# First loads, weight preparation and tail of an FFT-mix and top-1 MoE kernel: one constant moved to another queue, a software-pipelined Gram product, and the undecided tokens' list read in two blocks

## The chip, the cores and the metric

The kernel runs on one core of a Trainium2 chip. The metric is the device time of one execution in microseconds; three executions of the kernel before are given, and one of them was profiled. A smaller number is better.

## The reference

```python
X = np.fft.rfft(x, axis=1)                       # x: 8 x 3072 x 256
Yr, Yi = Xr @ w_r - Xi @ w_i + b_r, Xr @ w_i + Xi @ w_r + b_i
Yr, Yi = soft_threshold(Yr, 0.01), soft_threshold(Yi, 0.01)
t = np.fft.irfft(Yr + 1j * Yi, n=3072, axis=1)   # 24576 tokens of 256
r = np.maximum(t @ w_in, 0.0)                    # 256 x 2048
u = (s * (r * r) + b) @ w_out                    # 2048 x 256
e = argmax(u @ w_gate, axis=1)                   # 8 experts, softmax weight g
# each expert takes its first 768 tokens, in order; the others give 0
out[i] = g[i] * (np.maximum(u[i] @ w1[e], 0.0) @ w2[e])
```

The biases b_r and b_i are 64 times their usual size, so nearly all tokens choose the same expert. It is full after the first few hundred tokens, and most of the output is zero.

## The kernel before

**The body.** A batch of 3072 tokens is transformed as 32 x 96: `f1_items` multiplies 16 tiles of x by the matrix `f` (`pz`), writes the result `z` to the DRAM tensor `zd`, and `group_items` reads it back as `zp`, does the second half of the transform, the mix by `w_r` and `w_i` (`wm`) and the threshold. `i2_items` is the inverse transform (`pi`). Each token's row then goes to DRAM (`ad`) and through a first FFN in low precision (`ph`, `r`, `qb`, `lg`).

Which expert a token takes is computed exactly for the first 1024 tokens only. For all others `lg_set`, `lg_out` and `lg_fin` form bounds of the logits, and `decide_items(b)` finds the tokens of batch b whose bounds do not settle whether they go to the full expert. `to_list` writes their numbers to a DRAM list with eight indirect DMAs on POOL, appended to those of earlier batches (`base` is the count). `ovf` says that a batch had more of them in one row than the eight columns hold; in that case `whole_list` builds the whole list again, with 256 indirect DMAs (32 `to_list` steps for each batch).

**Weight preparation, before and in batch 0.** `conv_items(seq, ahead)` prepares the first FFN's weights in pieces: a load of `cr`, `conv_low` on ACT, `conv_use`/`conv_word` on DVE and POOL (`cf`), `conv_tr` (transposes `pwt`), `conv_gate` (`pg`). Pieces 0 to 7 (CONV_B) run among the first steps of batch 0. `gram_items` forms w_in times its transpose from the prepared weights, in 16 tiles: `turn(k, f)` transposes four 128x128 pieces (`pwg`) and ACT copies them to `wgt`; `add(k, f)` does four matmuls from `wgt` (`gram`). The items are put in slots of batch 0, at even distances up to GRAM_TO, in the order of this list:

```python
for k in range(2):
    for f in range(0, NF, 2):
        it += [lambda k=k, f=f: turn(k, f), lambda k=k, f=f: add(k, f)]
```

**First loads.** `run` issues the 16 loads of x for batch 0 on SP (`f1_load`, L214), then `load_consts` the constants, `f` first (L165), also on SP.

**The slots of a batch.** A batch's main loop has steps k; `slot` is a table from step number to work that is put in there. In the last batch it holds, from S_FROM = 27 to S_TO = 62, the sorting of the first 1024 tokens for the full expert, and at 62 `full_rows(j)`, the gathers of that expert's six blocks of 128 rows (`yf`).

**The tail.** Everything after the last batch stands in `tail`. `block(j)` is the full expert's block j: transposes `pt` (L1413), an ACT copy `yT`, 32 matmuls `ph` (L1423), 16 matmuls `po` (L1433), scatter `out` (L1438); its ten steps are [a, b x4, c x4, d]. `among(main, side)` spreads the steps of `side` among those of `main`. The order is: blocks 0 and 1 with `decide_items` of the last batch among them; `whole_list` (a branch on `ovf`, L884 and L888); `ids()`, which loads the list (`ci`) and makes row numbers of 512 entries on DVE (L1523 to L1532); four gathers `ga` of 128 rows (`x_load`); block 2; two parts (`e2_steps`) that recompute 256 listed tokens each exactly; block 3 with `xroute_items`, which counts them in; `e2_more`, which loads the list's count into a register and branches over a loop for lists of more than 512; blocks 4 and 5 with the tables of the other experts' tokens (`final_tables`, last `pit` and the cast `eo` on DVE, L1316). The loads of five experts' weights (`w`, `wb`, two `wq`, `wa`) and the gathers of their rows are issued from these. `regs()` then loads the two counts, and two nested chains of branches follow:

```python
with self.tc.If(self.nblk > n):    # item(n): block of 128 tokens of one expert
    ...
    if n + 1 < NI:
        self.item(n + 1)
with self.tc.If(self.nsml > NQ * g):  # small(g): three experts of up to 32
```

With these inputs items 0 and 1 and the group small(0) run. Matmuls on fp32 operands are used there. DRAIN instructions of every engine end the program (L1875).

## Time and profile before

| | |
|---|---|
| median of three executions | 1651.17 us (1646.57 to 1651.53) |
| profiled execution, its own time | 1647.89 us |
| its span | 1646.1 us |
| mean granted TensorE clock | 0.966 |
| TensorE busy (share of the span) | 89% |
| VectorE, ScalarE, GpSimd busy | 58%, 49%, 16% |

The span is the time from the first to the last instruction of the profiled execution. The shares are averages over stages that have different limits; so what a stage costs is read from its own waits and windows. A wait names the engine and line that stood still and what came last to release it. PEclk is the granted clock, 1.00 being 2.4 GHz and 0.50 1.2 GHz. "q" behind an engine's name is its sequencer, which runs branches, register loads and semaphores.

### The profile page before, as it was taken

To read this page: it belongs to the slowest core of one execution; us is meant where nothing else is said; L and a number is where in the kernel's file an instruction comes from. 1 tells how busy PE (TensorE), PEld (TensorE's weight loads), DVE (VectorE), ACT (ScalarE), POOL (GpSimd) and SP (SyncE) were. 2 spreads that over 40 slices of the span, in tenths; PEclk is the share of its full clock that TensorE was granted. 3 is DMA by queue.
4 is the path that set the end of the run, shared out by engine and by line. 5 is a ranking of instruction groups with operands and counts; after the bars stand their busy time and mean duration, and the time that the engine had idled before them with its cause. 6 is when DMAs were issued, how large, how long until landed. Compare 5 with 4: busy or idle time off the path is not lost. (4 is left out here: it accounts for less than half of the span.)

```text
span 1646.1 us, 26007 instructions
## 1 busy us (share of the span) xinstructions
PE 1471.8 (89%) x9469; PEld 1217.3 (74%) x9469; DVE 953.6 (58%) x2057; ACT 814.1 (49%) x1252; POOL 268.1 (16%) x235
## 2 busy tenths in 40 slices
PE   6986789999998799999999999999999988988865
PEld 3875568777877568867876887788688768977753
DVE  1856357645555767755765676577557686633510
ACT  1425544563334564476457446744764575632311
POOL 0534100110000040021012001300220161231020
PEclk9997999999999899999999999999999999999978
DMA  7635454562443365465446435644655347610035
GB/s 208 236 107 169 131 153 153 158 185 100 148 135 123 87 152 152 122 171 150 147 135 166 143 122 159 175 128 131 166 146 153 91 110 229 183 50 17 14 105 180
DMA packets 273572, 230.03 MB, mean 140 GB/s; under 512 B 120045, under 2 KB 228335, under 8 KB 273424
## 3 DMA queue, kind: packets, MB, share of 16 engines
q1 hardware_dynamic: 255776, 200.17, 42.5%
q10 hardware_dynamic: 13824, 25.17, 4.1%
q0 software_dynamic: 3824, 2.82, 0.7%
q8 instruction: 80, 1.31, 0.4%
q14 instruction: 68, 0.56, 0.1%
HBM read 114.18 MB, written 114.09 MB: 139 GB/s over the span
## 5 line engine op out<-in xcount | busy, mean ns | idle before, releaser
L723 PE MATMUL ph<-ah,win 128*128 128x384 f32 (+1 forms) x2048 | 489.5, 367 | 8.4 <-ACT r L728 7.8
L728 ACT ACTIVATE r<-ph 128x768 bf16<-128x768 f32 (+1 forms) x512 | 395.6, 784 | 165.9 <-PE ph L723 123.2
L729 DVE TENSOR_TENSOR qb<-r 128x768 bf16<-128x768 bf16 (+1 forms) x512 | 298.9, 585 | 298.2 <-ACT r L728 270.5
L723 PEld LDWEIGHTS ph<-ah,win 128*128 128x128 f32 x2048 | 344.9, 192 | 79.9 <-issue 41.6
L335 PE MATMUL pmx<-wm,l 128*128 128x256 f32 x1196 | 296.5, 386 | 17.1 <-DVE kb L345 9.6
L398 POOL TENSOR_TENSOR asq<-ah 128x768 bf16<-128x768 f32 x64 | 95.9, 1498 | 1045.7 <-ACT ah L394 967.5
L335 PEld LDWEIGHTS pmx<-wm,l 128*128 128x128 f32 x1196 | 220.9, 191 | 54.1 <-DVE kb L345 16.0
L392 PEld LDWEIGHTS pi<-f1t,u 96*128 96x128 f32 x1024 | 129.6, 196 | 17.8 <-issue 8.9
L392 PE MATMUL pi<-f1t,u 96*128 96x96 f32 x1024 | 134.1, 281 | 6.7 <-DVE l L262 4.3
L226 PE MATMUL pz<-x,f 96*96 96x512 f32 x240 | 126.6, 612 | 14.6 <-DMA f<-c_f 14.6
L261 ACT COPY l<-pf 128x512 f32<-128x512 f32 x84 | 49.2, 586 | 142.7 <-PE pf L253 142.3
L373 ACT COPY v<-pi 128x512 f32<-128x512 f32 x96 | 56.3, 587 | 125.5 <-PE pi L371 125.5
L371 PE MATMUL pi<-t,e 128*128 128x256 f32 x384 | 99.7, 383 | 5.2 <-DVE t L330 5.2
L253 PEld LDWEIGHTS pf<-d,zp 128*128 128x128 f32 x672 | 88.9, 193 | 11.6 <-issue 3.8
L253 PE MATMUL pf<-d,zp 128*128 128x128 f32 x672 | 90.0, 277 | 6.9 <-DMA zp<-zd 6.9
L408 DVE STREAM_TRANSPOSE at<-pi 128x384 f32<-128x384 f32 x128 | 74.1, 579 | 34.6 <-ACT ah L394 24.8
L394 ACT CAST ah<-pi 128x384 fp32r<-128x384 f32 x128 | 61.1, 479 | 57.3 <-PE pi L392 57.3
L234 ACT COPY z<-pz 96x512 f32<-96x512 f32 x120 | 69.8, 581 | 37.7 <-PE pz L226 29.8
L371 PEld LDWEIGHTS pi<-t,e 128*128 128x128 f32 x384 | 72.7, 191 | 17.6 <-DVE t L330 7.0
L330 DVE TENSOR_TENSOR t<-t,cl 128x512 f32<-128x512 f32 x96 | 72.1, 752 | 3.3
L877 POOL DMA_INDIRECT list<-c,x x64 | 65.9, 1029 | 45.1 <-DVE c L873 29.0
L759 ACT COPY ls<-lg 128x384 f32<-128x384 f32 (+1 forms) x64 | 52.8, 825 | 25.7 <-PE lg L746 15.5
(395 smaller groups left out, 1814.5 us busy)
## 6 DMA issues: line engine op xcount, KB each, us to landing
zd<-z SPq DMA_DIRECT2D x128, 192.0 KB
zp<-zd SPq DMA_DIRECT2D x96, 256.0 KB
vd<-v ACTq DMA_DIRECT2D x96, 256.0 KB
u<-vd SPq DMA_DIRECT2D x64, 384.0 KB
ad<-at SPq DMA_DIRECT2D x256, 96.0 KB
out<-zero SPq DMA_DIRECT2D x96, 256.0 KB
x<-x SPq DMA_DIRECT2D x120, 192.0 KB
sd<-stage SPq DMA_DIRECT2D x32, 256.0 KB
```

The costliest lines, as they stand in the source:

```text
L226: nc.tensor.matmul(o, self.f1, xs.rearrange("p a c -> p (a c)"), start=True, stop=True)
L234: nc.scalar.copy(out=z.rearrange("p a c -> p (a c)"), in_=o)
L253: nc.tensor.matmul(pv[:, h, :, gi * 64:gi * 64 + 64], zp[:, gi, h * 128:(h + 1) * 128], self.d[:, 2 * p + gi, :].rearrange("p (t m) -> p t ...
L330: nc.vector.tensor_tensor(out=t, in0=t, in1=cl, op=ALU.subtract)
L335: self.nc.tensor.matmul(o, part(h), w[:, h], start=start and h == 0, stop=stop and h == 1, skip_group_check=True)
L371: nc.tensor.matmul(ps[:, gi * C:(gi + 1) * C], self.e[:, 2 * p + gi], t[:, gi * C:(gi + 1) * C], start=True, stop=True)
L392: nc.tensor.matmul(ps[:, :TC].rearrange("p (a n) -> p a n", n=4)[:, :, n], u[:, n, h::2], self.f1t, start=True, stop=True)
L398: nc.gpsimd.tensor_tensor(out=self.asq[b, i], in0=af, in1=af, op=ALU.mult)
L408: nc.vector.transpose(out=self.ar[:, :, :, h], in_=self.at.pop((b, i, h))[:, :TC].rearrange("p (g c) -> p g c", c=32))
L723: nc.tensor.matmul(ps[:, j, :n], self.win[:, k, f], ah[:, k, t0:], start=(k == 0), stop=(k == 1))
L728: nc.scalar.activation(out=r, in_=ps[:, :, :n], func=AF.Relu)
L729: nc.vector.tensor_tensor(out=q, in0=r, in1=r, op=ALU.mult)
```

## The change

- `f` is loaded on ACT's queue, ahead of everything else, instead of on SP's behind x.
- `conv_items` gets a parameter `early`: for CONV_B the loads stand three steps ahead instead of two, and `conv_low` and `conv_word` two ahead instead of one. For this the buffer of `f` there takes turns with that of `t`.
- `gram_items`: `turn` of the next tile stands ahead of `add` of the one before; `wgt` has two buffers that take turns, and `gsq` another one.
- `first_block`, in slot 60 of the last batch, loads the first 256 entries of the list as they then are and gathers their rows (two `ga`). The tail begins with the recomputation of these (`part(0)`), with `decide_items` of the last batch among its steps. `whole_list` also rebuilds the list when fewer than 256 entries were there (`early`), and then does part 0 again (`redo`). The second 256 entries are gathered after it; block 0 and `part(1)` follow. The register load of `e2_more` goes ahead of block 0 (`e2_count`); its branch stays where `xroute_items` end.
- Blocks 1 and 2, and 3 to 5, are interleaved by `line`: the next block's first step goes ahead of this one's `po`.
- Items 0 and 1 (interleaved in the same way) and the first small group run without a branch; `regs()` and the chains of branches, from item 2 and from small group 1 on, come behind them.

The diff; in `small` the body is moved to `small_do` with the same lines, which are left out:

```diff
@@ -123,6 +123,7 @@
 S_FROM = 27
+LIST_AT = 60
 S_TO = 62
@@ -161,8 +162,6 @@
     def load_consts(self, cp):
         nc, I = self.nc, self.I
-        self.f1 = cp.tile([N1, 96], F32, tag="f1", name="f1")
-        nc.sync.dma_start(out=self.f1, in_=I["c_f1"])
         self.f1t = self.mo.tile([96, N1], F32, tag="f1t", name="f1t")
@@ -496,7 +495,7 @@
             pool = self.wk
-            tag, n = dict(t=("z", 4), p=("sl", 2), m=("v", 3), f=("zp", 3))[what]
+            tag, n = dict(t=("z", 4), p=("sl", 2), m=("v", 3), f=(("zp", "t")[k % 2], 3))[what]
         return pool.tile([128, 512], dt, tag=tag, name="c" + what, bufs=n)
     def conv_load(self, k):
@@ -583,18 +582,18 @@
-    def conv_items(self, seq, ahead):
+    def conv_items(self, seq, ahead, early=1):
         def at(f, n):
...
             at(self.conv_load, n + ahead)
-            at(self.conv_low, n + 1)
+            at(self.conv_low, n + early)
             for f, lag in ((self.conv_use, 0), (self.conv_tr, 1), (self.conv_gate, 2)):
...
                     f(seq[n - lag])
-            at(self.conv_word, n + 1)
+            at(self.conv_word, n + early)
         return [lambda n=n: step(n) for n in range(-ahead, len(seq) + (2 if seq[-1] < 8 else 0))]
     def load_bias(self, pp):
@@ -627,25 +626,27 @@
                                     (self.win, self.wl)[k].bitcast(F32)[:, c, (f + ff) * 128:(f + ff + 1) * 128], self.ident)
-            t = self.wk.tile([128, 2, 2 * 128], F32R, tag="kw", name="wgt", bufs=1)
+            t = self.wk.tile([128, 2, 2 * 128], F32R, tag=("kw", "kw2")[f // 2 % 2], name="wgt", bufs=1)
             nc.scalar.copy(out=t.rearrange("p a c -> p (a c)"), in_=ps)
-            self.wgt = t
+            self.wgt[k, f] = t
...
                 self.gram = self.lp.tile([128, 512], F32, tag="lg", name="gram")
+            t = self.wgt.pop((k, f))
             for ff in range(2):
                 for c in range(2):
-                    nc.tensor.matmul(self.gram[:, c * 256:(c + 1) * 256], self.wgt[:, ff, c * 128:(c + 1) * 128], self.wgt[:, ff],
+                    nc.tensor.matmul(self.gram[:, c * 256:(c + 1) * 256], t[:, ff, c * 128:(c + 1) * 128], t[:, ff],
                                      start=(f + ff == 0 and c == 0), stop=(f + ff == NF - 1), skip_group_check=True)
             if f == NF - 2:
-                sq = self.wk.tile([128, 512], F32, tag="kw2", name="gsq", bufs=1)
+                sq = self.wk.tile([128, 512], F32, tag="lh", name="gsq", bufs=2)
                 nc.scalar.activation(out=sq, in_=self.gram, func=AF.Square)
                 nc.vector.tensor_reduce(out=self.nrm[:, k:k + 1], in_=sq, axis=AX.X, op=ALU.add)
-        it = []
-        for k in range(2):
-            for f in range(0, NF, 2):
-                it += [lambda k=k, f=f: turn(k, f), lambda k=k, f=f: add(k, f)]
+        self.wgt = {}
+        tiles = [(k, f) for k in range(2) for f in range(0, NF, 2)]
+        it = [lambda: turn(*tiles[0])]
+        for n, t in enumerate(tiles):
+            it += [lambda u=u: turn(*u) for u in tiles[n + 1:n + 2]] + [lambda t=t: add(*t)]
         return it
     def bound_items(self, pp, diff=False):
@@ -802,7 +803,7 @@
         self.cnt, self.base = zero("cnt", [E]), zero("base", [1])
-        self.cmax = zero("cmax", [1])
+        self.cmax, self.early = zero("cmax", [1]), zero("early", [1])
         self.T = zero("T", [5, 48])
@@ -878,10 +879,13 @@
-    def whole_list(self):
+    def whole_list(self, redo):
         nc, V = self.nc, self.nc.vector
-        ovf = nc.values_load(self.ovf[0:1, 0:1], min_val=0, max_val=128)
+        V.tensor_scalar(out=self.early, in0=self.early, scalar1=float(TD), scalar2=None, op0=ALU.is_lt)
+        V.tensor_tensor(out=self.ovf, in0=self.ovf, in1=self.early, op=ALU.add)
+        ovf = nc.values_load(self.ovf[0:1, 0:1], min_val=0, max_val=129)
@@ -908,6 +912,7 @@
                     self.to_list(n, x, c)
+            redo()
     def x_load(self, ga, ids):
@@ -1443,76 +1448,81 @@
     def item(self, n):
         with self.tc.If(self.nblk > n):
-            if n > 1:
-                self.load_item(n)
-                self.rows(self.yr[n % 2], self.idy[:, n:n + 1])
-                self.gate(n)
-            for f in self.block_steps(self.wx[n % 2], self.yr[n % 2], self.gg[n % 2], self.ids[:, n:n + 1], "o2"):
+            self.load_item(n)
+            self.rows(self.yr[n % 2], self.idy[:, n:n + 1])
+            self.gate(n)
+            for f in self.item_steps(n):
                 f()
...
+    def item_steps(self, n):
+        return self.block_steps(self.wx[n % 2], self.yr[n % 2], self.gg[n % 2], self.ids[:, n:n + 1], "o2")
     def small_load(self, g, *qs):
...
     def small(self, g):
+        P = 32 * NQ
+        with self.tc.If(self.nsml > NQ * g):
+            self.small_load(g, *range(NQ))
+            self.rows(self.nr[:P], self.nids[:, 2, g:g + 1])
+            self.gather(self.ng[:P], self.gd, self.nids[:, 0, g:g + 1])
+            self.small_do(g)
+            if g + 1 < NS:
+                self.small(g + 1)
+    def small_do(self, g):
         nc, pq = self.nc, self.pq
...
@@ -1543,15 +1553,26 @@
-    def e2_more(self, p2, again):
-        nc, tc, V = self.nc, self.tc, self.nc.vector
-        bi, rem, blk = self.rt("e2i", [1], I32), self.rt("e2r", [1]), self.rt("e2b", [2])
+    def e2_count(self):
+        nc, V = self.nc, self.nc.vector
+        bi, rem = self.rt("e2i", [1], I32), self.rt("e2r", [1])
         V.tensor_scalar(out=rem, in0=self.base, scalar1=float(TD - 1), scalar2=None, op0=ALU.add)
...
         V.tensor_scalar(out=bi, in0=bi, scalar1=8, scalar2=None, op0=ALU.arith_shift_right)
-        n = nc.values_load(bi[0:1, 0:1], min_val=0, max_val=(self.B * S - XT) // TD)
+        self.nlist = nc.values_load(bi[0:1, 0:1], min_val=0, max_val=(self.B * S - XT) // TD)
+    def first_block(self):
+        c = self.e2_ids(2, self.list[0:TD], None, self.base)
+        self.nc.vector.tensor_copy(out=self.early, in_=self.base)
+        self.first_rows = self.x_load(self.gbuf[0], c[3])
+    def e2_more(self, p2, again):
+        nc, tc, V = self.nc, self.tc, self.nc.vector
+        rem, blk = self.rt("e2r", [1]), self.rt("e2b", [2])
+        n = self.nlist
         with tc.If(n > SB):
@@ -1610,33 +1631,40 @@
-        def load(k):
-            x[k] = self.x_load(self.gbuf[k % 2], x["c"][3][:, 2 * k:2 * k + 2])
         def among(main, side):
...
         self.lg_fin(B - 1, 7)
+        lg = self.rt("e2g", [2 * SB, E])
+        def part(k, rows):
+            return self.e2_steps(lambda: rows, lg, 2 * k, self.yx[XT + TD * k:XT + TD * (k + 1)])
+        def redo():
+            c = self.e2_ids(2, self.list[0:TD], None, self.base)
+            for f in part(0, self.x_load(self.gbuf[0], c[3])):
+                f()
+        def line(blocks):
+            it = [f for f in blocks[0][:5]]
+            for n, b in enumerate(blocks):
+                nx = blocks[n + 1] if n + 1 < len(blocks) else []
+                it += nx[:1] + b[5:] + nx[1:5]
+            return it
         blocks = [block(j) for j in range(NJ)]
-        among(blocks[0] + blocks[1], self.decide_items(B - 1))
-        self.whole_list()
+        among(part(0, self.first_rows), self.decide_items(B - 1))
+        self.whole_list(redo)
         ids()
-        for k in range(min(SB, 2)):
-            load(k)
-        lg = self.rt("e2g", [2 * SB, E])
-        for f in blocks[2]:
+        rows = self.x_load(self.gbuf[1], x["c"][3][:, 2:4])
+        self.e2_count()
+        for f in blocks[0] + part(1, rows):
             f()
-        for k in range(SB):
-            st = self.e2_steps(lambda k=k: x[k], lg, 2 * k, self.yx[XT + TD * k:XT + TD * (k + 1)])
-            st.pop(0)()
-            if k + 2 < SB:
-                load(k + 2)
-            for f in st:
-                f()
         hf, lf, val, row = x["c"]
         side = self.xroute_items(2 * SB, lg, lambda: hf, lambda: lf, lambda: x["b"], self.gdv[:, XB:XB + 2 * SB], val)
-        among(blocks[3], side)
+        among(line(blocks[1:3]), side)
@@ -1646,10 +1674,13 @@
         self.wx = [self.wx[1], cut(wb)]
-        among(blocks[4] + blocks[5], tables)
+        among(line(blocks[3:]), tables)
+        for f in line([self.item_steps(n) for n in range(2)]):
+            f()
+        self.small_do(0)
         regs()
-        self.item(0)
-        self.small(0)
+        self.item(2)
+        self.small(1)
     def run(self):
@@ -1687,6 +1718,8 @@
             nc.vector.memset(zero, 0.0)
+            self.f1 = cp.tile([N1, 96], F32, tag="f1", name="f1")
+            nc.scalar.dma_start(out=self.f1, in_=self.I["c_f1"])
             for t in range(16):
@@ -1714,7 +1747,7 @@
                 if not conv:
-                    conv = self.conv_items(CONV_B, 2)
+                    conv = self.conv_items(CONV_B, 3, 2)
             self.warm(WARM_GROUPS)
@@ -1779,6 +1812,7 @@
                     slot.setdefault(S_TO, []).extend(lambda j=j: self.full_rows(j) for j in range(NJ))
+                    slot.setdefault(LIST_AT, []).append(self.first_block)
                     self.yf = [p2.tile([128, C], F32, tag=f"yf{j}", name=f"yf{j}") for j in range(NJ)]
...
```

TensorE where the Gram product begins in batch 0 (`ph` is the first FFN, `pwt` a transposition of `conv_tr`), before:

```order
L723 MATMUL ph<-ah,win 128x256 x4
L569 MATMUL pwt<-ident,cf 128x128 x4
L628 MATMUL pwg<-ident,win 128x128 x4
L639 MATMUL gram<-wgt 128x256 x4
L628 MATMUL pwg<-ident,win 128x128 x4
L639 MATMUL gram<-wgt 128x256 x4
L723 MATMUL ph<-ah,win 128x256 x4
```

and with the change:

```order
L724 MATMUL ph<-ah,win 128x256 x4
L627 MATMUL pwg<-ident,win 128x128 x8
L639 MATMUL gram<-wgt 128x256 x4
L627 MATMUL pwg<-ident,win 128x128 x4
L724 MATMUL ph<-ah,win 128x256 x4
L568 MATMUL pwt<-ident,cf 128x128 x4
L639 MATMUL gram<-wgt 128x256 x4
L627 MATMUL pwg<-ident,win 128x128 x4
```

The eight transposes at the start are those of two tiles. From there on each group of four Gram matmuls has the transposes of the next tile ahead of it, where before its own stood directly ahead.

VectorE at the register load of the list's count, before (`T` is the last step of `xroute_items`, L1120):

```order
L1120 TENSOR_TENSOR T<-ptb,T 128x240
L1551 TENSOR_SCALAR e2r<-base 128x1
L1552 CAST e2i<-e2r 128x1
L1553 TENSOR_SCALAR e2i<-e2i 128x1
L1554 TENSOR_LOAD e2i
L1555 COMPARE_AND_BRANCH
```

and with the change, behind the row numbers of the list (`xd` is the first step of `part(1)`):

```order
L1539 CAST clf_16289<-cl_16284 128x4
L1540 SCALAR_TENSOR_TENSOR crf_16291<-clf_16289,chf_16288 128x4
L1541 CAST cw_16285<-crf_16291 128x4
L1542 TENSOR_SCALAR cva_16290<-c_dd,base 128x4
L1632 TENSOR_SCALAR e2p<-c_x 128x4
L1559 TENSOR_SCALAR e2r<-base 128x1
L1560 CAST e2i<-e2r 128x1
L1561 TENSOR_SCALAR e2i<-e2i 128x1
L1562 TENSOR_LOAD e2i
L930 TENSOR_TENSOR xd<-pt,xd 128x512
```

The count and its load have moved from behind the last step of `xroute_items` to ahead of the second part; the branch on it is not among these rows any more.

GpSimd behind the gathers of the other experts' rows and gates (`ints` holds the two counts), before:

```order
L1395 DMA nr<-zd,idn 96x256
L1395 DMA ng<-gd,idn 96x1
L1335 TENSOR_LOAD ints
L1336 TENSOR_LOAD ints
L1445 COMPARE_AND_BRANCH
L1438 DMA out<-o_17537,idi 24576x256
L1445 COMPARE_AND_BRANCH
```

and with the change:

```order
L1400 DMA nr<-zd,idn 96x256
L1400 DMA ng<-gd,idn 96x1
L1443 DMA out<-o_17849,idi 24576x256
L1443 DMA out<-o_17883,idi 24576x256
L1523 DMA out<-o_17978,idn 24576x256
L1340 TENSOR_LOAD ints
L1341 TENSOR_LOAD ints
L1450 COMPARE_AND_BRANCH
```

The three scatters stand ahead of the two register loads, and the first branch follows these.

## Rows read from the trace of the kernel before

**Rows 1.** The page's part 1: busy time, share of the span, instructions of each engine.

```profile
PE 1471.8 (89%) x9469; PEld 1217.3 (74%) x9469; DVE 953.6 (58%) x2057; ACT 814.1 (49%) x1252; POOL 268.1 (16%) x235
```

**Rows 2.** Timeline of SP's issues: start us, us, what. First 37 us.

```profile
9.85 0.31 SPq L165 DMA_DIRECT2D f<-c_f  x1
...
35.63 0.84 SPq L242 DMA_DIRECT2D zp<-zd  x2
```

**Rows 3.** Timeline of PE, start to first group; in brackets the idle time before.

```profile
14.56 3.73 PE L226 MATMUL pz<-x,f 96*96 96x512 f32 x4 [14.56 <-DMA f<-c_f]
...
30.72 7.93 PE L420 MATMUL warm<-zero 128*128 128x256 f32 x36
38.55 0.68 PE L280 MATMUL pf<-d,zp 128*128 128x128 f32 x4
```

**Rows 4.** Windows, start: us; busy of PE, PEld, DVE, ACT, POOL; PEclk; DMA share; GB/s.

```profile
0.00:4.50 4.50, 0.00 (x0) 0.00 (x0) 0.44 (x4) 1.28 (x1) 1.75 (x10) 1.00 0.50 150
4.50:14.50 10.00, 0.00 (x0) 0.00 (x0) 0.00 (x0) 0.00 (x0) 0.00 (x0) 1.00 0.96 255
```

**Rows 5.** Waits of PE from 106 to 190 us: total, times, longest.

```profile
PE gram L639 <- ACT wgt L631: 16.0, 12, 8.0
PE pwt L569 <- POOL cf L552: 2.0, 1, 2.0
```

**Rows 6.** Windows of the weights' stage.

```profile
134.00:152.00 18.00, 13.80 (x108) 11.62 (x108) 8.23 (x16) 9.47 (x19) 7.63 (x6) 0.68 0.48 162
152.00:162.00 10.00, 8.41 (x69) 6.86 (x70) 9.03 (x13) 5.20 (x10) 5.87 (x5) 0.66 0.38 127
```

**Rows 7.** Windows of the tail.

```profile
1490.56:1523.00 32.44, 29.59 (x231) 26.23 (x232) 11.50 (x18) 10.30 (x18) 2.80 (x3) 0.95 0.06 17
1523.00:1553.10 30.10, 28.23 (x233) 24.62 (x232) 12.44 (x20) 10.29 (x18) 0.00 (x0) 1.00 0.03 10
1591.50:1624.30 32.80, 17.64 (x106) 15.47 (x110) 0.69 (x5) 4.29 (x9) 8.19 (x9) 0.78 0.98 341
...
1634.36:1646.10 11.74, 0.00 (x0) 0.00 (x0) 0.00 (x0) 0.00 (x0) 0.94 (x1) 0.62 0.03 8
```

**Rows 8.** Waits of PE in the tail, 1456 to 1646.1 us.

```profile
PE pt L1413 <- DMA yr<-zd,idi: 7.6, 1, 7.6
PE pt L1413 <- DVE k L1291: 6.5, 1, 6.5
PE pt L1470 <- ACTq L1445: 6.0, 1, 6.0
PE ph L1423 <- ACT yT L1415: 3.9, 7, 0.7
...
PE pt L923 <- DMA ga<-ad,cw: 2.2, 2, 1.4
PE ph L1423 <- issue: 2.1, 1, 2.1
...
PE pt L1413 <- PEq L888: 1.3, 1, 1.3
PE pt L1413 <- DMA yf<-zd,f_y: 1.1, 1, 1.1
```

**Rows 9.** Sequencer instructions of three lines: duration ns min/median/max, first and last start.

```profile
L1555 PEldq COMPARE_BRANCH  x1: 4235/4235/4235, 1566.4 to 1566.4; - x1
...
L1445 PEldq COMPARE_BRANCH  x4: 65/138/6424, 1591.6 to 1621.0; - x4
...
L1445 POOLq INC_SWDGE_SEM  x1: 2106/2106/2106, 1623.8 to 1623.8; - x1
...
L1875 POOLq DRAIN  x3: 46/103/8161, 1637.1 to 1645.8; - x3
```

**Rows 10.** List's DMAs on POOL: duration ns min/median/max, first and last start.

```profile
L877 POOL DMA_INDIRECT list<-c,x x8: 919/920/926, 1470.5 to 1480.4; - x8
```

**Rows 11.** Timeline of PE, last matmuls of the small group that read wa.

```profile
1631.42 1.05 PE L1497 MATMUL po<-wa,hT 128*32 128x256 f32 x16
```

More of the change, by code (lines that the diff above doesn't have):

```diff
@@ new lines, in small_do, with first @@
+        pt = pq.tile([128, 512], F32, tag="py", name="pt4", bufs=4)
+        for h in range(2):
+            nc.tensor.transpose(pt[:, h * P:(h + 1) * P], self.nr[:P, h * 128:(h + 1) * 128], self.ident[:P, :P])
+        yT = self.pb.tile([128, 2, P], F32, tag="yT", name="yT", bufs=2)
+        nc.scalar.copy(out=yT.rearrange("p h c -> p (h c)"), in_=pt[:, :2 * P])
+        hs, hT, os = {}, {}, {}
+        def first(n):
+            ps = pq.tile([128, 512], F32, tag="h", name="ph4", bufs=3)
+            for h in range(2):
+                for j in range(4):
+                    nc.tensor.matmul(ps[32 * j:32 * j + 32, :C], yT[:, h, 32 * n:32 * n + 32],
+                                     self.wq[n][0][:, h, C * j:C * (j + 1)], start=(h == 0), stop=(h == 1),
+                                     skip_group_check=True)
+            hs[n] = self.pb.tile([128, 2, 128], F32, tag="yT", name="hs", bufs=2)
+            nc.scalar.activation(out=hs[n].rearrange("p c f -> p (c f)"), in_=ps[:, :C], func=AF.Relu)
@@ new lines, in turn, with second @@
+        def turn(n):
+            pt = pq.tile([128, 512], F32, tag="py", name="pt5", bufs=4)
+            for c in range(2):
+                nc.tensor.transpose(pt[:, c * 128:(c + 1) * 128], hs[n][:, c], self.ident)
+            hT[n] = self.pb.tile([128, 2, 4, 32], F32, tag="xq", name="hT", bufs=4)
+            nc.vector.tensor_copy(out=hT[n].rearrange("p c j t -> p (c j t)"), in_=pt[:, :C])
+        def second(n):
+            po = pq.tile([128, 512], F32, tag="py", name="po4", bufs=4)
+            for c in range(2):
+                for j in range(4):
+                    nc.tensor.matmul(po[32 * j:32 * j + 32, :C], hT[n][:, c, j], self.wq[n][1][:, 2 * j + c],
+                                     start=(c == 0), stop=(c == 1), skip_group_check=True)
+            os[n] = self.pb.tile([128, C], F32, tag=("eh", "el", "y")[n], name="os", bufs=(2, 2, 1)[n])
+            nc.scalar.copy(out=os[n], in_=po[:, :C])
@@ new lines, in small_do @@
+        for n in range(NQ + 3):
+            for f, k in ((first, 0), (turn, 1), (second, 3)):
+                if 0 <= n - k < NQ:
+                    f(n - k)
+        pr = pq.tile([128, 512], F32, tag="py", name="pr4", bufs=4)
+        for n in range(NQ):
+            nc.tensor.matmul(pr[32 * n:32 * n + 32, :C], self.sel, os[n], start=True, stop=True,
+                             skip_group_check=True)
+        o = self.pb.tile([128, C], F32, tag="o4", name="o4", bufs=1)
+        nc.scalar.activation(out=o[:P], in_=pr[:P, :C], func=AF.Copy, scale=self.ng[:P])
@@ L1518, in e2_ids @@
+        nc.gpsimd.indirect_dma_start(
+            out=self.out, out_offset=bass.IndirectOffsetOnAxis(ap=self.nids[:, 1, g:g + 1], axis=0),
+            in_=o[:P], in_offset=None, bounds_check=self.B * S - 1, oob_is_err=False)
     def e2_ids(self, M, src, start, rem):
@@ L1824, in run @@
                             todo += self.decide_items(fb)
+                    assert b < B - 1 or k < LIST_AT or not todo
                     if todo:
```

48 lines of the change are left out of this document (removed).

## The prediction

> **What bounds the kernel now.** I read the page first. TensorE is busy for 89% of the 1646.1 us span [rows 1], so the body of the kernel can only be shortened by taking matmuls away, and the change takes none away. What it can win are the stretches in which TensorE stands still or runs at the lower clock. The waits and the windows show three such places, and the change has a part for each.
>
> At the start TensorE does nothing for 14.56 us. What ends this is the constant f, a 36 KB matrix, which SP issues at 9.85, as the 17th load, behind sixteen of x [rows 2, 3].
>
> Between 124 and 190 us the weights are prepared: transposes (pwg), an ACT copy (wgt), Gram matmuls. The Gram matmuls wait 12 times for that copy, 16.0 us in all, 8.0 of it in one wait [rows 5]; the other eleven share the rest, 0.73 each. With these gaps the granted clock stood at 0.68 and 0.66 from 134 to 162 us [rows 6], between the levels 1.2 and 2.4 GHz.
>
> In the tail (from 1456) TensorE waits 6.5 us for the tables behind e2_more's branch, 7.6 for the rows of the first item, 6.0 before small, and stands still for the last 11.74 us [rows 7, 8].
>
> **Sum, against the profiled execution (1647.89 us, of which the span is 1646.1).** The median of the three runs is 1651.17, 3.3 above it, so 3.3 is added at the end. A change under 0.3% (5 us) can't be told from none.
>
> *Start.* f goes to ACT's queue as its first instruction, and can be issued near 0.8 instead of 9.85. In the trace it took 4.7 us from issue to use, with the DMA engines 0.96 busy [rows 2, 3, 4], so it is there by some 5.5, or earlier, as the engines are half as busy up to 4.5. The first x, 0.2 MB, is in by then: 150 GB/s up to 4.5 are 0.7 MB [rows 4]. TensorE then starts near 4.5 and its 16.16 us (14.56 to 30.72) end near 20.7 in place of 30.72. What comes next is bound by traffic: x (16 loads of 192 KB), z written back (16 of 192 KB), d and wm, together 7.3 MB, at the 255 GB/s of that window [rows 4] 28.6 us, ending near 29.4; zp is issued once the last z landed, 35.63 before, and the groups begin 2.9 us after [rows 2, 3]. Traffic alone would let zp start at 29.4 (gain 6); TensorE alone near 25.6, as the last z needs 4.9 us from the end of its matmul to zp here too (gain 10). I take 8, between the two, as neither waits for the other all the time: **-8** (-6 to -10). f1t and the small MoE constants are one slot earlier and SP has one issue less: nothing. ACT's table load is pushed behind one issue of about 0.4; it is needed only when the first pz is there.
>
> *Weights.* One more tile of transposes goes ahead of each group of Gram matmuls, with a second buffer for wgt, so TensorE has four transposes to run during an ACT copy: the eleven waits of 0.73 go, -8. conv_low and conv_word run a step earlier: the wait of pwt for cf, 2.0 [rows 5], goes too. The single long wait has another cause, the ACT queue held by a load of cr, and stays. Late next is DVE, which is busy 9.03 of 10 us from 152 to 162 [rows 6]: there TensorE can't get much ahead, and the whole 28 us from 134 to 162 hold 17.3 of DVE and 14.7 of ACT. [...] The conversions get one step more, and pb, the matmul behind them, may wait 1 longer. I take -10 + 1: **-9** (-3 where DVE binds, -14 where the clock also recovers).
>
> *Tail up to the item numbers (cast at 1591.50).* Before, two full-expert blocks covered the decisions, one covered the list's load; now the first part of the undecided tokens covers the decisions, and nothing covers the list. Removed: e2_more's count and its register load, about 2.2 of its 6.5 us; TensorE's own branch of 4.24 [rows 9] stays. The wait for rows ga, 2.2, and for the branch at whole_list, 1.3 and 2.1 [rows 8]. The part 0 that ran cold, 32.44 against 30.10 at the full clock [rows 7]: -2.3. Interleaving drops the wait of ph for yT three times, 0.55 each [rows 8]: -1.7. The first wait for yf, 1.1. That is -12.9. Added: after part 0 nothing else can run while DVE forms the flag, every engine loads ovf and branches, POOL resets its DMA semaphores (about 2 [rows 9]), SP loads the list (some 2), DVE makes addresses (1) and the count, and every engine loads that too. Nearest is e2_more's pause of 6.5; with the list's load it is 8.6, less the 0.7 that a block's start has anyway: +7.9. The other end is 4 (all engines ready) and 13 (a 4.2 branch in the chain, not beside it). Sum **-5** (-10 to 0). The two gathers that move into the last batch take POOL about 1 us each, as the list's DMAs do [rows 10], ahead of yf, and are hidden by that batch's matmuls; without this cover part 0 would start up to 2.2 late.
>
> *Items and small.* The items and the first small group run without branches between them, so the 6.0 before small goes, and 0.7 of the second block's start. But the experts' weights keep the DMA engines busy, 0.98, until about 1624 [rows 7], 32.5 us after the cast, and their last use, from po on, is 3 us before the last scatter [rows 7, 11]. The last scatter came 42.9 after the cast (1634.36 [rows 7]); without the two gaps it comes after 36.2, and the weights allow 35.5: **-7** (-4 to -8).
>
> *End.* Registers are loaded after the last scatter instead of before the items. Behind that scatter there were 11.74 us [rows 7], with small's exit and a DRAIN of 8.16 [rows 9]; now the loads, the item chain's branch F and its reset of POOL's semaphores, 2.1 [rows 9], come ahead of these. Loads and semaphores I put at 1.6, an estimate from e2_more's pause without its branch, 6.5 - 4.24 = 2.3, less DVE's arithmetic in it. The item chain's branch took 6.42 on PE [rows 9], beside full DMA traffic; e2_more's took 4.24 with quiet DMA. I take F = 4: **+7.7** (+3.8 where F is 0.1, +9 near 5.3; less where the DRAIN finds less to wait for).
>
> Rule against row: of the four branches on the item line three took 65 to 138 ns on PE and one 6424, and e2_more's took 4235 [rows 9]; I expect a long one, since the skipped code is as far. By the Trainium skill (Advanced Engine Details and Errata, Control Flow Timing) a compare-and-branch is about 108 ns, which would make the end +3.8 and the total 1626; the same skill (Runtime: NRT & Kernel Launch, Instruction fetch mechanics) says that a taken branch to a target outside the loaded pages waits for a fetch, with which the two long rows agree.
>
> Sum: -8 - 9 - 5 - 7 + 7.7 = -21.3, so 1647.9 - 21.3 + 3.3 = **1630 us**.
>
> **Rivals.** (a) *The start is not carried through.* The f load lands with x's backlog, near 14, whichever queue issues it. For: the DMA engines were 0.96 busy from 4.5 on. Against: f needed only 4.7 us there, behind 16 loads of x; ahead of them it has nothing to wait for. Then the first term is 0: 1638. The Trainium skill (DMA: Bandwidth & Descriptors, Issuing engines are not separate DMA queues) says that transfers of all issuing engines share the same DMA engines and that a second issuer saves only issue time; no trace so far shows f on another queue. (b) *DVE binds the weights stage.* For: 9.03 of 10 [rows 6]. Against: only in that window; the term is then -3: 1636. (c) *The exits are cheap*, like the branches of 65 to 138 ns, or the DRAIN is shorter because less is in flight. For: no weights are in flight there any more. Against: e2_more's long branch had none beside it either. The end is +3.8 or less: 1626 and below. (d) *Slower: the list is short.* If it holds fewer than 256 tokens when slot 60 reads the count, whole_list rebuilds it, with 256 indirect DMAs. Eight of them, with a scatter between, started over 9.9 us [rows 10], 1.23 apart; so 315 us, and part 0 again, 30: about 1975. It decides at 256. Against: the inputs, put through the kernel's own bounds, give about 430 undecided tokens after seven batches of eight and 491 at the end, and before's loop over further blocks did not run. (e) *The list pause costs 13 and the other far branches grow too*, as redo puts a whole part behind whole_list's branch: the tail is 0 and the end +9. For: two long branches in the trace. Against: both were on PE alone, beside the chain. 1636.
>
> **How the numbers follow.** My sum 0.50, (a) 0.13, (b) 0.15, (c) 0.10, (e) 0.10, (d) 0.02. The bounds of the unknown terms, not all at their ends at once, give -36 to -9 for all but (d): 1615 to 1642. All of these but (d) are faster by over 5 us, and only several bad ends together come within it: faster 0.93, same 0.05, slower 0.02.
>
> **What would show it.** TensorE's first matmul near 4.5, the groups' first near 30.5; Gram waits of about 8 in place of 16.0, with the granted clock over 0.75 in that stage; one TensorE gap of 8 to 10 us behind part 0, one of about 4.3 at e2_more; no gap before small; from the last scatter to the end 19 us in place of 11.74. I am wrong if f is still the last to arrive, if the gap behind part 0 passes 13, or if list DMAs by the hundred stand in the tail.

## The result, and the profile after

The changed kernel takes 1639.8 us (median of six; 1634.1 to 1641.6), against 1651.4 for the kernel before in the same runs. The ratio is 0.9915 (95% interval 0.9887 to 0.9943), 14 us less, between 9 and 19 (the two medians lie 11.6 apart). The prediction of 1630 us had the sign right and was 10 us too fast; its range, 1615 to 1642, holds the time near its slow end. The profiled execution has a span of 1632.1 us, against 1646.1: 14.0 less too, so the two traces can be compared row by row.

I cut both spans at the same instructions. The timeline of TensorE in the kernel before, besides [rows 3] the first Gram matmul, the norm's matmul pnr and the last transposes of the bounds (plt), after which the tail begins:

```profile
134.10 1.23 PE L639 MATMUL gram<-wgt 128*128 128x256 f32 x4 [8.00 <-ACT wgt L631]
...
191.78 0.39 PE L690 MATMUL pnr<-nrm,ones 128*128 128x4 f32 x2 [1.35 <-DVE ones L688]
...
1456.66 0.64 PE L767 MATMUL plt<-ident,ls 128*96 128x128 f32 x4 [0.91 <-ACT ls L759]
```

The same of the changed kernel, with the rows that answer to [rows 3]:

```profile
4.07 3.73 PE L225 MATMUL pz<-x,f 96*96 96x512 f32 x4 [4.07 <-DMA f<-c_f]
...
20.48 7.93 PE L419 MATMUL warm<-zero 128*128 128x256 f32 x36
31.22 0.68 PE L279 MATMUL pf<-d,zp 128*128 128x128 f32 x4 [2.81 <-issue]
...
125.45 1.22 PE L639 MATMUL gram<-wgt 128*128 128x256 f32 x4 [6.35 <-ACT wgt L630]
...
174.81 0.39 PE L691 MATMUL pnr<-nrm,ones 128*128 128x4 f32 x2 [1.35 <-DVE ones L689]
...
1441.00 0.64 PE L768 MATMUL plt<-ident,ls 128*96 128x128 f32 x4 [0.91 <-ACT ls L760]
```

The cast of the item numbers (timeline of VectorE) and the last scatter (timeline of GpSimd) of the changed kernel; before they were at 1591.50 and 1634.36 [rows 7]:

```profile
1573.99 0.20 DVE L1321 CAST eo<-pit 1x51 int32<-1x51 f32 x1 [25.91 <-PE pit L1318]
```

```profile
1613.90 0.95 POOL L1523 DMA_INDIRECT out<-o,idn  x1 [13.45 <-ACT o L1522]
```

| from, to | before | after | difference | forecast |
|---|---|---|---|---|
| start to first group | 38.55 | 31.22 | -7.3 | -8 |
| to the first Gram matmul | 95.55 | 94.23 | -1.3 | 0 |
| to pnr | 57.68 | 49.36 | -8.3 | -9 |
| to plt (the batches) | 1264.88 | 1266.19 | +1.3 | 0 |
| to the item numbers' cast | 134.84 | 132.99 | -1.9 | -5 |
| to the last scatter | 42.86 | 39.91 | -3.0 | -7 |
| to the end | 11.74 | 18.20 | +6.5 | +7.7 |
| sum | 1646.10 | 1632.10 | -14.0 | -21.3 |

The start and the weights gave nearly what was forecast. The tail was forecast at -5 - 7 + 7.7 = -4.3; it gave +1.6, which one pair of profiles does not tell from nothing: from plt to the end the four kernels with the old tail took 189.4 to 192.9 us, and the three with the changed tail (the one without redo among them) 188.5 to 191.1. Its largest waits are these (waits of TensorE from 1425 us on):

```profile
PE pt L1418 <- DVE e2i L1561: 11.4, 1, 11.4
PE pt L1418 <- DMA yr<-zd,idi: 7.0, 1, 7.0
PE pt L1418 <- DVE k L1296: 5.2, 1, 5.2
PE ph L1492 <- SPq L1450: 4.2, 1, 4.2
```

The first is the pause behind part 0, the recomputation of the first 256 tokens. It was forecast at 8.6, and 11.4 were measured. The second and third answer to the first two of [rows 8]. The 6.0 in front of small is gone, and 4.2 have come in its place.

### The profile page after: what moved, and what is told of

It reads as the page before. It is cut to its first block, busy times and chain, and to the rows that moved or that the text cites. A ratio compares the mean times of both kernels' runs of the same rounds, so it can differ in the third digit from the quotient of the medians.

```text
span 1632.1 us, 26008 instructions
## 1 busy us (share of the span) xinstructions
PE 1466.2 (90%) x9469; PEld 1217.0 (75%) x9469; DVE 958.4 (59%) x2068; ACT 814.2 (50%) x1252; POOL 268.7 (16%) x235
## 5 line engine op out<-in xcount | busy, mean ns | idle before, releaser
L391 PEld LDWEIGHTS pi<-f1t,u 96*128 96x128 f32 x1024 | 131.3, 199 | 17.7 <-issue 9.1
L370 PEld LDWEIGHTS pi<-t,e 128*128 128x128 f32 x384 | 72.2, 190 | 17.3 <-DVE t L329 7.0
```

The costliest lines, as they stand in the source:

```text
L370: nc.tensor.matmul(ps[:, gi * C:(gi + 1) * C], self.e[:, 2 * p + gi], t[:, gi * C:(gi + 1) * C], start=True, stop=True)
L391: nc.tensor.matmul(ps[:, :TC].rearrange("p (a n) -> p a n", n=4)[:, :, n], u[:, n, h::2], self.f1t, start=True, stop=True)
```

## The experiments

Twelve kernels were run, in three groups. The batches between pnr and plt, where only slot 60 of the last batch has new work, took 1262 to 1273 us in the profiles of these runs. So a change of 2 or 3 us is read from a stage, not from the total.

**The three parts alone.** First f on ACT's queue, in the kernel before:

```diff
-        nc.sync.dma_start(out=self.f1, in_=I["c_f1"])      # in load_consts
+            nc.scalar.dma_start(out=self.f1, in_=self.I["c_f1"])   # in run, ahead of f1_load
```

> The kernel before with one edit: f goes on ACT's queue. Theory (the terms are independent and the start is carried through): TensorE's first matmul near 4.1 instead of 14.56, groups from about 31.2 instead of 38.55, and every later landmark earlier by 7 to 9 us, so 8 us faster (ratio 0.995). Rival (DMA traffic or a later wait takes it back): first matmul early, but the groups or the first matmul of the inverse transform (121.93 before) within 3 us of before, ratio 0.998 or more.

Measured: ratio 0.9964 (0.9943 to 0.9986), 6 us faster. The timeline of TensorE:

```profile
3.72 3.73 PE L224 MATMUL pz<-x,f 96*96 96x512 f32 x4 [3.72 <-DMA f<-c_f]
...
30.89 0.68 PE L278 MATMUL pf<-d,zp 128*128 128x128 f32 x4 [2.89 <-issue]
```

The groups begin at 30.89, 7.7 earlier, and the inverse transform's first matmul is at 114.69 instead of 121.93. The rival falls: the gain is carried through. The 8 us that were expected lie within the interval (2 to 9 us).

Then the edits of the weight preparation alone (gram_items and conv_items as in the diff, the rest as before):

> The kernel before with the weight preparation's edits alone (next tile's transposes ahead of the Gram matmuls, two buffers, conversions a step earlier). Theory: from the first Gram matmul to the norm's matmul pnr 49.4 us as in the changed kernel instead of 57.7, with Gram waits of about 7 instead of 16.0, so 8 us faster (ratio 0.995). Rival (the gain needs the earlier start, since DVE and ACT have then other work beside): 53 us or more, 4 us faster or less.

Measured: ratio 0.9940 (0.9918 to 0.9961), 10 us faster; from the first Gram matmul to pnr 50.1 us. So the gain does not need the earlier start. And of these edits the Gram product alone, with conv_items as it was:

```diff
-                    conv = self.conv_items(CONV_B, 3, 2)
+                    conv = self.conv_items(CONV_B, 2)
```

> The kernel before with the pipelined Gram product alone, the conversions as before. Theory (the eleven waits of 0.73 are the term, and the conversions' wait for cf is 2): from the first Gram matmul to pnr 57.7 falls to 51 to 52, with the waits of pwt for cf left; 6 us faster, ratio 0.996. Rival (the copies' two buffers help only where the conversions are ahead): 55 or more, 2 us faster or less.

Measured: ratio 0.9924 (0.9903 to 0.9945), 12 us faster, the stage 47.0 us. TensorE's waits between 95 and 195 us with both edits:

```profile
PE gram L640 <- ACT wgt L631: 7.5, 2, 7.2
PE pwg L628 <- DVE wog L584: 2.6, 2, 2.0
```

and with the Gram product alone:

```profile
PE gram L640 <- ACT wgt L631: 7.4, 2, 7.1
PE pwt L569 <- POOL cf L552: 5.3, 3, 3.8
```

Without the early conversions pwt waits for cf, 5.3 us in three waits; with them TensorE waits at pwg, pwt and pg for wog, DVE's copy of the gate products. The two kernels' intervals overlap. The earlier conversions move a wait from one engine's tile to another's; a gain of theirs is not seen. With both edits the stage took 47.9 to 50.1 us in ten profiles.

The tail alone, on the start and weights of before:

> The changed kernel with the start and the weight preparation as before: only the tail's edits. Theory from the two traces: from the last plt of the bounds to the item numbers' cast 1.9 us shorter, from there to the last scatter 3.0 shorter, from it to the end 6.5 longer: no change within the noise, 1.7 us slower (ratio 1.001). Rival (my sum: the tail as predicted, and the trace of the changed kernel happened on a bad one): 4 us faster (0.9975), TensorE's gap behind part 0 under 10 us.

Measured: ratio 1.0000 (0.9977 to 1.0023). From plt to the cast 131.3, from there to the last scatter 39.9, to the end 17.3; the pause behind part 0 is 11.0. The rival, 4 us faster, falls: the tail's edits gain and lose the same. The three parts alone sum to -6 - 10 + 0 = -16, within the noise of the -14 of the whole.

**What the pause behind part 0 is made of.** The count's register load is moved behind block 0:

```diff
+        for f in blocks[0]:
+            f()
         self.e2_count()
-        for f in blocks[0] + part(1, rows):
+        for f in part(1, rows):
             f()
```

> The changed kernel with the register load of the list's count moved behind block 0, ahead of part 1. Theory (behind part 0 TensorE waits for the load of a count that needs no TensorE, its own branch is over 6 us earlier): the gap behind part 0 falls from 11.4 to about 5.3, block 0 runs beside the list's load, and about 0.5 comes back at the moved load; 5 to 6 us faster than the changed kernel, ratio to before 0.988. Rival (the rows of part 1 are then the last to arrive): the gap shrinks, but part 1 waits for ga by as much, and the time stays at the changed kernel's.

Measured: ratio 0.9876 (0.9838 to 0.9915), 20 us faster than before the change and 6 faster than the change by the ratios, whose intervals overlap. From plt to the cast 127.4 us, 5.6 less than in the changed kernel; but part 0 was also faster in this profile (31.2 instead of 32.6). In the run of the tail alone part 0 took 31.2 too, and against that the stage is 3.8 shorter. In TensorE's waits of the tail the 11.4 have become:

```profile
PE pt L1418 <- PEq L892: 5.8, 1, 5.8
```

That wait ends with TensorE's own branch. The rival falls: TensorE does not wait for the rows of part 1. Then redo is left out of whole_list, which makes the code that TensorE skips short (the rare path is incomplete; these data do not take it):

```diff
-            redo()
```

> The changed kernel without redo in whole_list (a part of the rare path is left out; the data don't take it). Theory (the gap behind part 0 is a chain over POOL: branch, reset, list load, DVE; TensorE's long branch lies beside it): TensorE's branch falls from 3627 ns to some 240, the gap stays at 11 to 11.5, the time at the changed kernel's. Rival (TensorE's branch is in the chain, as my range for the pause allowed): the gap falls by 3 or more, ratio to before 0.9895.

Measured: ratio 0.9921 (0.9895 to 0.9947), as the changed kernel. The sequencer's rows of the branch and TensorE's wait behind part 0:

```profile
L892 POOLq EVENT_SEMAPHORE  x4: 17/43/43, 1485.6 to 1485.9; - x4
...
L892 POOLq COMPARE_BRANCH  x1: 53/53/53, 1482.8 to 1482.8; - x1
L892 PEldq COMPARE_BRANCH  x1: 228/228/228, 1482.8 to 1482.8; - x1
...
L892 POOLq INC_SWDGE_SEM  x1: 1820/1820/1820, 1486.0 to 1486.0; - x1
```

```profile
PE pt L1417 <- DVE e2i L1560: 10.8, 1, 10.8
```

TensorE's branch fell from 3627 to 228 ns, and the pause only from 11.4 to 10.8. So it was not TensorE's branch that set it. The rows of the same line in the changed kernel (instructions, min/median/max ns, first and last start):

```profile
L892 POOLq EVENT_SEMAPHORE  x4: 17/43/43, 1479.3 to 1479.5; - x4
...
L892 POOLq COMPARE_BRANCH  x1: 53/53/53, 1476.0 to 1476.0; - x1
L892 PEldq COMPARE_BRANCH  x1: 3627/3627/3627, 1476.0 to 1476.0; - x1
...
L892 POOLq INC_SWDGE_SEM  x1: 1820/1820/1820, 1479.6 to 1479.6; - x1
```

POOL's branch has a row of 53 ns at 1476.0, but its next instruction starts at 1479.3, 3.3 us later. Then comes the reset of its DMA semaphores, 1.8, to 1481.4, and SP issues the list's load at 1481.65, right behind it. POOL is on the path here, as the forecast's sum said; the 3.3 us behind its branch were not in it, since the row shows only 53 ns. In the six profiles with the count ahead of block 0 that gap was 2.8, 2.9, 3.1, 3.3, 3.6 and 3.7 us, and the pause, in the same order, 10.8, 11.0, 11.3, 11.4, 11.7 and 11.8: the one follows the other. The trace of before had it already, at the same branch:

```profile
L888 POOLq EVENT_SEMAPHORE  x4: 17/42/43, 1481.9 to 1482.2; - x4
...
L888 POOLq COMPARE_BRANCH  x1: 53/53/53, 1479.4 to 1479.4; - x1
```

There the gap is 2.5 us, and the list's load is issued at 1484.46, behind a reset of 1.8. What the pause would be with both edits, the count behind block 0 and short skipped code, was not run.

**The end.** The rare items and groups under one branch, on a flag that DVE forms with the tables:

```diff
-        regs()
-        self.item(2)
-        self.small(1)
+        with tc.If(self.more() > 0):
+            regs()
+            self.item(2)
+            self.small(1)
```

> The changed kernel with the register loads, the items from 2 on and the small groups from 1 on put under one branch on a flag that DVE forms with the tables. Theory (each exit behind the last scatter costs the branch's fetch and a reset of POOL's semaphores, one after the other): one reset, one branch and one load go, from the last scatter to the end 15.3 in place of 18.2, 3 us faster than the changed kernel. Rival (the final DRAIN ends at a time set by the scatter's landing): 18.2 stays.

Measured: ratio 0.9913 (0.9890 to 0.9937), in the total no difference from the changed kernel; from the last scatter to the end 15.7 instead of 18.2. POOL's rows of the one branch:

```profile
L1689 POOLq EVENT_SEMAPHORE  x5: 17/43/43, 1621.9 to 1622.2; - x5
...
L1689 POOLq COMPARE_BRANCH  x1: 45/45/45, 1618.6 to 1618.6; - x1
...
L1689 POOLq INC_SWDGE_SEM  x1: 2131/2131/2131, 1622.3 to 1622.3; - x1
```

Behind the branch 3.3 us pass without a row, as at the first of the changed kernel's two exits; one reset is saved. Then the items and small under their branches as before, registers ahead:

```diff
-        for f in line([self.item_steps(n) for n in range(2)]):
-            f()
-        self.small_do(0)
         regs()
-        self.item(2)
-        self.small(1)
+        self.item(0)
+        self.small(0)
```

> The changed kernel with items 0 and 1 and the first small group under their branches again, registers loaded ahead, no interleaving of the items, as before the change. Theory from the two traces: cast to last scatter 42.9 in place of 39.9, last scatter to end 11.7 in place of 18.2: 3.5 us faster than the changed kernel, ratio to before 0.9895. Rival (my forecast: the freed branch gives 7 where all else is equal): slower than the changed kernel by what the scatter comes later than 43.

Measured: ratio 0.9889 (0.9855 to 0.9923); cast to last scatter 43.0, scatter to end 11.8, together 3.3 less than the 58.1 of the changed kernel. The old wait in front of small is there again, 5.5 us. The total is 4 us lower by the ratios, which their intervals do not tell apart; by the stages the old end is the better one. And one branch ahead of the weight loads, none at the end (in final_tables, ahead of the gathers of item 0):

```diff
+            with self.tc.If(nc.values_load(v["more"][0:1, 0:1], min_val=0, max_val=NI + E) > 0):
+                r()
+                self.item(2)
+                self.small(1)
             self.rows(self.yr[0], self.idy[:, 0:1])
```

> The changed kernel with one branch for the rare items and groups, placed ahead of the loads of items 0, 1 and small group 0, none behind the last scatter. Theory (the branch's fetch and the reset of POOL are hidden while the weights load, and the end then holds the scatter and the DRAIN alone): from last scatter to end 10 in place of 18.2; cast to scatter 39.9 plus what SP's branch delays the weights, 1 to 4; 4 to 7 us faster than the changed kernel. Rival (the weights are delayed by a branch of 4 and a reset of 2): 46 to the scatter, 2 us faster.

Measured: ratio 0.9924 (0.9895 to 0.9952); scatter to end 9.9, as expected, and cast to scatter 42.7. TensorE waits twice as long for item 0's rows, 14.2 us instead of 7.0, since POOL gathers them behind its branch and reset. The two stages gain 5.5 (52.6 instead of 58.1). The total does not show it: in this profile the tail began at 1446.8, 5.8 later than in the changed kernel's, and took 2.6 longer to the cast, with a part 0 of 35.4.

**A better version.** In the changed kernel six table steps were spread over blocks 3 to 5, so the item numbers came when these blocks were done, and the last stage waited for rows and weights. The steps need nothing of the blocks. In the next run they are put ahead of and beside block 3; the count stays behind block 0:

```diff
-        among(line(blocks[3:]), tables)
+        ta, td, te, td1, tf, tg = tables
+        for f in (ta, td, te, tf):
+            f()
+        for n, f in enumerate(line(blocks[3:])):
+            f()
+            for k, g in ((2, td1), (8, tg)):
+                if n == k:
+                    g()
```

> The changed kernel with the count behind block 0, and the other experts' tables formed beside block 3 instead of spread over blocks 3 to 5. Theory (the item numbers need nothing of these blocks, and the last stage waits for rows, 7.0, for weights, 4.2, and starts cold): the cast comes some 17 us before the blocks end, the waits of 7.0 and 4.2 go, the last scatter comes 10 to 12 us earlier relative to the bounds' plt than with the count alone; 16 to 17 us faster than the changed kernel, ratio 0.981. Rival (the weight loads beside the blocks delay them, or DVE's tables hold up block 3): half of it or less, ratio over 0.984.

Measured: ratio 0.9798 (0.9778 to 0.9817), 33 us faster than before the change. Plt to last scatter takes 151.2 us, against 168.0 with the count alone and 172.9 in the changed kernel. That is 16.8 less than with the count alone, where 10 to 12 were expected: the waits of 7.0 and 4.2 are gone, and the granted clock from the cast to the last scatter is 1.00, where in the changed kernel it was 0.84 to 1606 and 0.78 behind it. What each gave is not taken apart. With the one branch at the end as well:

> The one before with the rare items and groups under one branch. Theory: from the last scatter to the end 15.7 instead of 18.2, as in the run with one exit alone; ratio 0.9795. Rival: the exits overlap with something else now, 18.2 stays.

Measured: **1615.6 us, ratio 0.9774 (0.9755 to 0.9793)**, 37 us faster than before the change; scatter to end 14.4, with a gap of 2.6 behind POOL's branch. The interval overlaps that of the run before it. TensorE's timeline at item 0's first transposes and at the first use of wa, and a window of that stage:

```profile
1573.37 0.38 PE L1426 MATMUL pt<-ident,yr 128*128 128x128 f32 x2
...
1592.97 1.07 PE L1500 MATMUL ph<-wa,yT 128*32 128x256 f32 x16
```

```profile
1575.00:1590.00 15.00, 14.62 (x100) 13.65 (x100) 0.00 (x0) 3.45 (x8) 2.66 (x3) 1.00 1.05 379
```

Neither row has a wait any more, and the granted clock is 1.00, the level of 2.4 GHz, while the DMA engines are full (1.05, 379 GB/s). Last, the one branch behind block 3, ahead of the loads:

> The changed kernel with the count behind block 0, the tables beside block 3, and the rare items' and groups' one branch behind block 3, ahead of the weight loads. Theory (nothing behind the last scatter but the DRAIN; POOL's reset and fetch lie beside blocks 4 and 5, TensorE's own fetch of about 4 does not): last scatter to end 9.9 instead of 18.2, one TensorE gap of 4 to 7 more; 19 to 21 us faster than the changed kernel, ratio 0.979. Rival (the branch delays the weights by 6 and the scatter with them): no better than the one exit at the end, 0.981.

Measured: ratio 0.9792 (0.9774 to 0.9810). Scatter to end 9.9, but from plt to the scatter 157.5 instead of 153.2: the branch, at which TensorE waits 3.6, and block 3 that is not interleaved with the next, cost together what the end gains. From plt to the end both take 167.5 us. The rival is right here: not better than one exit at the end.

## Why the prediction was right, and where not

**Start: right.** f, issued first on ACT's queue, was there at 4.07. zp was issued at 28.46, between the bounds of TensorE alone (25.6) and of traffic (29.4), and the DMA engines were full until 18 us. SP's issues, and windows:

```profile
20.04 5.43 SPq L235 DMA_DIRECT2D zd<-z  x8
28.46 0.84 SPq L241 DMA_DIRECT2D zp<-zd  x2
```

```profile
4.50:14.50 10.00, 10.00 (x19) 3.42 (x18) 2.75 (x4) 2.33 (x4) 0.00 (x0) 1.00 1.03 277
14.50:18.00 3.50, 3.50 (x10) 1.37 (x9) 1.38 (x2) 1.16 (x2) 0.00 (x0) 1.00 1.01 256
18.00:33.00 15.00, 12.19 (x59) 9.36 (x58) 1.38 (x2) 1.39 (x3) 0.00 (x0) 1.00 0.82 273
```

Rival (a) falls: f did not wait for x's backlog. The Trainium skill (DMA: Bandwidth & Descriptors, Issuing engines are not separate DMA queues) is not against this: what ACT's queue saved is SP's issue at 9.85, behind sixteen loads, and the shared engines are seen in the traffic bound.

**Weights: right in size, not in its parts.** Of the eleven short waits one of 0.3 is left, and the long one fell from 8.0 to 6.4. The wait for cf is down to 0.3 too, but TensorE waits for wog in its place, 5.4 in all, which I had put at nothing (waits of TensorE, 95 to 185 us):

```profile
PE gram L639 <- ACT wgt L630: 6.7, 2, 6.4
...
PE pwt L568 <- DVE wog L583: 2.0, 1, 2.0
PE pg L581 <- DVE wog L583: 1.8, 1, 1.8
...
PE pwg L627 <- DVE wog L583: 1.6, 1, 1.6
```

Windows of the stage, of the same lengths as in [rows 6]:

```profile
125.45:143.45 18.00, 13.93 (x147) 12.53 (x148) 14.21 (x22) 13.40 (x25) 9.61 (x8) 0.88 0.67 232
143.45:153.45 10.00, 8.41 (x55) 7.70 (x54) 8.24 (x11) 3.32 (x6) 6.42 (x6) 0.54 0.35 116
```

The clock rose to 0.88 in the first, and was at 0.54 in the second, which follows two of these waits and holds the third. DVE was busy 8.24 of 10 us there. So rival (b) is part of the truth: DVE is what is late next. The -2 for the conversions is not borne out, as the Gram product alone gave as much (47.0 us); nor did the +1 at pb come (1.7 before, 1.6 after). And no run shows the -14 with a recovered clock: over the 28 us of these two windows its mean rose from 0.67 to 0.76, and the stage became 10.6 us shorter at most, in the run with the Gram product alone.

**Tail to the cast: the pause was mis-sized.** I took 8.6 for it, with an upper end of 13 for a branch "in the chain, not beside it". The branch in the chain is POOL's, with 3.3 us behind it, and the list pause was 10.8 to 11.8 in all the runs that have the count ahead of block 0. The row it was sized from, e2_more's pause, has no such gap on POOL, whose next row came there 0.4 us behind its branch. The row of whole_list's own branch, 2.5 us, would have been the nearer one. About half of the pause is a wait for the count, which TensorE does not need there: with the load behind block 0 it is 5.8. From e2_more's pause 1.3 went (6.5 to 5.2), where I had 2.2. A second step failed in this profile: part 0 was not warm. It took 32.6 us, as before, and began at a clock of 0.79 (window of its first 8 us):

```profile
1441.50:1449.50 8.00, 7.10 (x46) 6.26 (x44) 3.23 (x6) 2.40 (x4) 4.81 (x5) 0.79 0.30 98
```

In the ten profiles with this code it took between 31.2 and 36.0. In five of them the clock of its first 8 us was 1.00, and it took 31.2 to 31.3; it was 0.79 where it took 32.6 and 33.1, and 0.57 and 0.58 where it took 35.9 and 36.0. (In the tenth, the run with the early exit, it was 1.00 too, but 0.85 at the end of part 0, which took 35.4.) In all ten TensorE was busy for 8.5 of the 10 us ahead of part 0, at 1.00. So the -2.3 for it was not there in this profile, at most half of it came in others, and what decides between them stays open.

**Items and small: the weights' bound was too low.** I let the weights' last use, from po on, be 3 us before the last scatter. But the wait is at wa's first use, ph. Its row in the trace of before, and in the changed kernel:

```profile
1627.73 1.07 PE L1480 MATMUL ph<-wa,yT 128*32 128x256 f32 x16
```

```profile
1605.97 1.23 PE L1492 MATMUL ph<-wa,yT 128*32 128x256 f32 x16 [4.18 <-SPq L1450]
```

Before, it was 6.6 ahead of the last scatter, so my bound would have been 32.5 + 6.6 = 39.1; now it is 32.0 behind the cast, and the scatter 7.9 behind it, 39.9 in all. The row names SP's sequencer; in the run without redo the same wait, 3.8, is put down to the DMA of wa, and the DMA engines' share falls at 1606 from 0.98 to 0.11. The 7.0 for item 0's rows was known and stayed. The last scatter came 39.9 after the cast, where I had 36. The run with the early tables shows the mechanism: both waits go.

**End: right in size, by another engine's branch.** +6.5 against +7.7. The exits stand one after the other (sequencer rows; first and last start):

```profile
L1450 POOLq EVENT_SEMAPHORE  x4: 17/43/43, 1618.1 to 1618.3; - x4
...
L1450 PEldq COMPARE_BRANCH  x1: 3884/3884/3884, 1613.3 to 1613.3; - x1
...
L1450 POOLq COMPARE_BRANCH  x1: 45/45/45, 1614.7 to 1614.7; - x1
...
L1450 POOLq INC_SWDGE_SEM  x1: 2131/2131/2131, 1618.4 to 1618.4; - x1
...
L1469 PEldq COMPARE_BRANCH  x1: 3207/3207/3207, 1617.4 to 1617.4; - x1
...
L1469 POOLq INC_SWDGE_SEM  x1: 2132/2132/2132, 1621.0 to 1621.0; - x1
...
L1910 POOLq DRAIN  x3: 46/108/8072, 1623.2 to 1631.8; - x3
```

POOL's branch at 1614.7 is followed by 3.4 us without a row, then a reset of 2.1 and the second exit with a reset of 2.1; the DRAIN is 8.07 where it was 8.16 [rows 9]. TensorE's two branches, 3.9 and 3.2, lie beside this. The loads, part of the 1.6 in the sum, came to 0.8 (1613.90 to 1614.7). I had F = 4 from TensorE's rows; what stands in the chain is POOL's gap of 3.4, so that the two are alike in size is luck. Rival (c) falls. The Trainium skill (Runtime: NRT & Kernel Launch, Instruction fetch mechanics) says that a taken branch to code outside the loaded pages waits for a fetch; TensorE's rows agree: 3.6 us over the long skipped code of whole_list, 0.23 where it was made short. POOL's gap of 3.3 to 3.4 us behind a row of 45 to 53 ns could be the same thing by its length; no run here tells a fetch from another cause of that gap.

**Rivals (d) and (e).** There are 64 list DMAs in the trace, eight for each batch, as before: whole_list did not run, so the list had its 256 tokens. (e) is what happened in half: the pause came over half the way to its upper end, the end did not.

## What to carry to other kernels

A register load on every engine is a barrier also for the engine that has nothing to do with the register: put it where the latest of its producers is long done. A branch that guards rare code can cost a gap and a reset on POOL, which issues DMAs (here 2.5 to 3.7 and about 2 us), so put such code under one flag, and compare the places for its branch by the whole stage: here the branch ahead of the last loads came out as the one behind the last scatter (167.5 us from plt to the end). And before work is interleaved to hide a wait, look whether what is waited for could simply be asked for earlier, as here the tables, which were worth more (17 us from plt to the last scatter) than the other edits of the tail together.

## What the runs showed of the hardware

- A branch's row can hide its cost. At whole_list and at the first exit behind the last scatter POOL's row has 45 to 53 ns, and its next row comes 2.5 to 3.7 us later in the profiles read. This is not so at every branch: at e2_more's it comes within 0.5 us, at the second exit within 0.2. TensorE's own rows of the branches over long code have 2.9 to 5.0 us in the changed kernel and its variants.
- The DRAIN of POOL at the end took 8.07 to 8.16 us in all profiles with a branch's exit behind the last scatter, whether the last scatter lay 12 or 18 us before the end. In the two without one it took 9.26, with the scatter's own 0.95 in it. So some 8 us behind the last scatter are left whatever stands there.
- Part 0, with the same code and order, took 31.2 to 36.0 us in ten profiles; the granted clock of its first 8 us was 1.00 in six of them, 0.79 in two and 0.57 and 0.58 in two.
